# Two products of a dense SiLU layer computed transposed, with 512 moving columns, through DRAM scratch and transposing loads, with one pool of eight PSUM banks

## The chip, the cores and the metric

One core of a Trainium2 chip. The time is the device time of one execution in microseconds (us); the profile is one such execution, and its span (320.8 us before) is a little shorter than the time (322.6 us), because the time also holds what lies around the traced instructions. PE is TensorE; PEld is its loading of stationary operands; ACT is ScalarE, DVE is VectorE; SP is the engine whose queue issues nearly all DMA transfers of this kernel, in order.

## The reference

```python
def _fwd_reference(x, w1, w2):            # x [1, 2048, 640], w1 [640, 1536], w2 [1536, 640], bf16
    h = jnp.einsum("bsd,df->bsf", x, w1)
    h = _silu(h)
    return jnp.einsum("bsf,fd->bsd", h, w2)

def reference(x, w1, w2, grad_out):       # returns out, grad_x, grad_w1, grad_w2
    _out, _vjp = jax.vjp(_fwd_reference, x, w1, w2)
    return (_out, *_vjp(grad_out))
```

There are six matrix products: h = x w1, g = grad_out w2^T, out = silu(h) w2, grad_x = gh w1^T, grad_w2 and grad_w1.

## The kernel before

The sequence is worked through in four chunks of 512 rows. In a chunk, h and g are computed transposed (F on the partitions, 512 rows of the sequence moving), giving `aT` and `ghT`. Then `sd_phase` makes out and grad_x of the chunk: a 128x128 piece of `aT` or `ghT` is stationary and 320 columns of `w2` or of `w1` transposed move. At the end two phases compute the weight gradients from `a_blk` and `gh_blk`, which are `aT` and `ghT` written to DRAM scratch and loaded back transposed.

```python
    P = 128                                # S, D, F = 2048, 640, 1536
    SC, FC, DH = 512, 512, D // 2          # ST, DT, FT = 16, 5, 12 blocks of 128
    abpool = ...                           # bufs=1: a_blk 0
    ps_h = ctx.enter_context(tc.tile_pool(name="ps_h", bufs=4, space=PSUM))   # one bank each
    ps_o = ctx.enter_context(tc.tile_pool(name="ps_o", bufs=2, space=PSUM))   # two banks each
    # ... first loads; 36 warm-up matmuls; chunk 0 of x is transposed on PE ...

        def sd_phase(c, lhs_all, rhs_all, dst_v, on_act):
            o_sb = opool.tile([P, STC, D], dt_in, name="o_sb")
            for sl in range(STC):                              # 4 blocks of rows
                op_ = ps_o.tile([P, 2, 512], FP32, name="op")
                for ft in range(FT):                           # 12
                    for hf in range(2):
                        nc.tensor.matmul(
                            op_[:, hf, 0:DH],
                            lhsT=lhs_all[:, ft, sl * P:(sl + 1) * P],
                            rhs=rhs_all[:, ft, hf * DH:(hf + 1) * DH],
                            start=(ft == 0), stop=(ft == FT - 1),
                        )
                # evicted by ACT (out) or DVE (grad_x) to o_sb
            nc.sync.dma_start(out=dst_v[:, c * STC:(c + 1) * STC, :], in_=o_sb[:])

        for c in range(NCH):
            # ... h and g groups, 5 matmuls of 512 columns each, 12 + 12 groups ...
            # aT, ghT -> aT_scr, ghT_scr
            if c == NCH - 1:
                load_a_blk(0, abpool)                          # transposing load
            sd_phase(c, aT, w2_nat, out_v, True)
            sd_phase(c, ghT, w1T, gx_v, False)

    with ExitStack() as fctx:                                  # last phases
        # fpool, gbpool, s1pool, ab2pool, in this order
        for fc in range(1, NFC):
            load_a_blk(fc, ab2pool)
        # three transposing loads of gh_blk, then grad_w2 (240 matmuls) and grad_w1
```

Of the kernel before, what the change touches and what calls it, by code (L numbers as in the profile page):

```python
# [8 lines left out]
ACT = mybir.ActivationFunctionType  # L9
ALU = mybir.AluOpType  # L10
FP32 = mybir.dt.float32
# [4 lines left out]
def kernel(  # L16
# [11 lines left out]
    nc = tc.nc  # L28
    P = 128
# [6 lines left out]
    S, D = x2.shape  # L36
    F = w1.shape[1]
    ST, DT, FT = S // P, D // P, F // P
    SC = 512
    NCH = S // SC  # L40
    STC = SC // P
    DH = D // 2
    FC = 512
    NFC = F // FC
    LAG = 2
    NWARM = 36
    dt_in = x.dtype

    dram = ctx.enter_context(tc.tile_pool(name="dram", bufs=1, space=bass.MemoryType.DRAM))
    natpool = ctx.enter_context(tc.tile_pool(name="natpool", bufs=1))  # L50
    abpool = ctx.enter_context(tc.tile_pool(name="abpool", bufs=1))
    ps_h = ctx.enter_context(tc.tile_pool(name="ps_h", bufs=4, space=bass.MemoryType.PSUM))
    ps_o = ctx.enter_context(tc.tile_pool(name="ps_o", bufs=2, space=bass.MemoryType.PSUM))

    aT_scr = dram.tile([F, S], dt_in, name="aT_scr")
    ghT_scr = dram.tile([F, S], dt_in, name="ghT_scr")
    g2T_scr = dram.tile([D, F], dt_in, name="g2T_scr")

    go_nat = natpool.tile([P, ST, D], dt_in, name="go_nat")
# [6 lines left out]
    out_v = out2.rearrange("(st p) d -> p st d", p=P)  # L66
    gx_v = gx2.rearrange("(st p) d -> p st d", p=P)

    a_blks = []

    def load_a_blk(fc, pool):
        a_blk = pool.tile([P, ST, FC], dt_in, name="a_blk")
        nc.sync.dma_start_transpose(out=a_blk[:], in_=aT_scr[fc * FC:(fc + 1) * FC, :])
        a_blks.append(a_blk)

    with ExitStack() as mctx:
        cpool = mctx.enter_context(tc.tile_pool(name="cpool", bufs=1))
        wpool = mctx.enter_context(tc.tile_pool(name="wpool", bufs=1))
# [3 lines left out]
        opool = mctx.enter_context(tc.tile_pool(name="opool", bufs=2))  # L82
# [9 lines left out]
        ident = cpool.tile([P, P], dt_in, name="ident")  # L92
        make_identity(nc, ident[:])

        w1_nat = wpool.tile([P, DT, F], dt_in, name="w1_nat")
        w2_nat = wpool.tile([P, FT, D], dt_in, name="w2_nat")
        w1T = wpool.tile([P, FT, D], dt_in, name="w1T")
        w2T = wpool.tile([P, DT, F], dt_in, name="w2T")

        def load_xT(c):  # L100
            xT = xpool.tile([P, DT, SC], dt_in, name="xT")
            nc.sync.dma_start_transpose(out=xT[:], in_=x2[c * SC:(c + 1) * SC, :])
            return xT

        def load_goT(c):
            goT = xpool.tile([P, DT, SC], dt_in, name="goT")
            nc.sync.dma_start_transpose(out=goT[:], in_=go2[c * SC:(c + 1) * SC, :])
            return goT
# [51 lines left out]
        def g_group(ft, goT, ghT):  # L160
            gp = ps_h.tile([P, SC], FP32, name="hp")
            for dt_ in range(DT):
                nc.tensor.matmul(  # L163
                    gp[:],
                    lhsT=w2T[:, dt_, ft * P:(ft + 1) * P],
                    rhs=goT[:, dt_, :],
                    start=(dt_ == 0),
                    stop=(dt_ == DT - 1),
                )
            nc.vector.scalar_tensor_tensor(  # L170
                out=ghT[:, ft, :], in0=ghT[:, ft, :], scalar=1.0, in1=gp[:], op0=ALU.add, op1=ALU.mult
            )

        def sd_phase(c, lhs_all, rhs_all, dst_v, on_act):
            o_sb = opool.tile([P, STC, D], dt_in, name="o_sb")
            for sl in range(STC):
                op_ = ps_o.tile([P, 2, 512], FP32, name="op")
                for ft in range(FT):
                    for hf in range(2):
                        nc.tensor.matmul(  # L180
                            op_[:, hf, 0:DH],
                            lhsT=lhs_all[:, ft, sl * P:(sl + 1) * P],
                            rhs=rhs_all[:, ft, hf * DH:(hf + 1) * DH],
                            start=(ft == 0),
                            stop=(ft == FT - 1),
                        )
                dst = o_sb[:, sl, :].rearrange("p (h d) -> p h d", h=2)
                if on_act:
                    nc.scalar.activation(dst, op_[:, :, 0:DH], ACT.Copy)  # L189
                else:  # L190
                    nc.vector.tensor_copy(out=dst, in_=op_[:, :, 0:DH])  # L191
            nc.sync.dma_start(out=dst_v[:, c * STC:(c + 1) * STC, :], in_=o_sb[:])

        for c in range(NCH):
            xT, goT = xT_next, goT_next
            aT = apool.tile([P, FT, SC], dt_in, name="aT")
            ghT = apool.tile([P, FT, SC], dt_in, name="ghT")

            if c + 1 < NCH:
                xT_next = load_xT(c + 1)  # L200
                goT_next = load_goT(c + 1)
            if c == 1:
                for j in range(0, ST, STC):
                    nc.sync.dma_start(out=go_nat[:, j:j + STC, :], in_=go_v[:, j:j + STC, :])
            if c == 2:
                for j in range(STC, ST, STC):
                    nc.sync.dma_start(out=x_nat[:, j:j + STC, :], in_=x_v[:, j:j + STC, :])

            if c == 0:
                for ft in range(FT):  # L210
                    h_group(ft, xT, aT, ghT)
                nc.sync.dma_start(
                    out=aT_scr[:, c * SC:(c + 1) * SC].rearrange("(ft p) s -> p ft s", p=P), in_=aT[:]
                )
                sd_phase(c, aT, w2_nat, out_v, True)
                for ft in range(FT):
                    g_group(ft, goT, ghT)
                nc.sync.dma_start(
                    out=ghT_scr[:, c * SC:(c + 1) * SC].rearrange("(ft p) s -> p ft s", p=P), in_=ghT[:]
                )  # L220
                sd_phase(c, ghT, w1T, gx_v, False)
                continue

            for i in range(FT + LAG):
                if i < FT:
                    h_group(i, xT, aT, ghT)
                if i >= LAG:
                    g_group(i - LAG, goT, ghT)

            nc.sync.dma_start(  # L230
                out=aT_scr[:, c * SC:(c + 1) * SC].rearrange("(ft p) s -> p ft s", p=P), in_=aT[:]
            )
            nc.sync.dma_start(
                out=ghT_scr[:, c * SC:(c + 1) * SC].rearrange("(ft p) s -> p ft s", p=P), in_=ghT[:]
            )
            if c == NCH - 1:
                load_a_blk(0, abpool)

            sd_phase(c, aT, w2_nat, out_v, True)
            sd_phase(c, ghT, w1T, gx_v, False)  # L240

    with ExitStack() as fctx:
        fpool = fctx.enter_context(tc.tile_pool(name="fpool", bufs=NFC))
        gbpool = fctx.enter_context(tc.tile_pool(name="gbpool", bufs=NFC))
        s1pool = fctx.enter_context(tc.tile_pool(name="s1pool", bufs=3))

        ab2pool = fctx.enter_context(tc.tile_pool(name="ab2pool", bufs=NFC - 1))
        for fc in range(1, NFC):
            load_a_blk(fc, ab2pool)
        gh_blks = []  # L250
        for fc in range(NFC):
            gh_blk = gbpool.tile([P, ST, FC], dt_in, name="gh_blk")
            nc.sync.dma_start_transpose(out=gh_blk[:], in_=ghT_scr[fc * FC:(fc + 1) * FC, :])
            gh_blks.append(gh_blk)

        gw2_v = gw2.rearrange("(ft p) d -> p ft d", p=P)
        g2T_v = g2T_scr[:].rearrange("(dt p) f -> p dt f", p=P)
# [2 lines left out]
        for fc in range(NFC):  # L260
            a_blk = a_blks[fc]
            g2T = fpool.tile([P, DT, FC], dt_in, name="g2T")
            for dt_ in range(DT):
                gp = ps_h.tile([P, FC], FP32, name="hp")
                for st in range(ST):
                    nc.tensor.matmul(  # L266
                        gp[:],
                        lhsT=go_nat[:, st, dt_ * P:(dt_ + 1) * P],
                        rhs=a_blk[:, st, :],
                        start=(st == 0),  # L270
                        stop=(st == ST - 1),
# [15 lines left out]
        for fc in range(NFC):  # L287
            gh_blk = gh_blks[fc]
            for dt_ in range(DT):
                if dt_ == DT // 2:  # L290
                    store_gw2(fc)
                if fc == NFC - 1 and dt_ == DT - 1:
                    for k, (lo, hi) in enumerate(((0, FC - P), (FC - P, FC))):
                        gp = ps_h.tile([P, FC], FP32, name="hp")
                        for st in range(ST):
                            nc.tensor.matmul(  # L296
                                gp[:, lo:hi],
                                lhsT=x_nat[:, st, dt_ * P:(dt_ + 1) * P],
                                rhs=gh_blk[:, st, lo:hi],
                                start=(st == 0),  # L300
                                stop=(st == ST - 1),
# [4 lines left out]
                        else:  # L306
                            nc.vector.tensor_copy(out=g1[:, lo:hi], in_=gp[:, lo:hi])  # L307
                        nc.sync.dma_start(
                            out=gw1_v[:, dt_, fc * FC + lo:fc * FC + hi], in_=g1[:, lo:hi]
# [3 lines left out]
                for st in range(ST):  # L313
                    nc.tensor.matmul(  # L314
                        gp[:],
                        lhsT=x_nat[:, st, dt_ * P:(dt_ + 1) * P],
                        rhs=gh_blk[:, st, :],
                        start=(st == 0),
                        stop=(st == ST - 1),
# [38 lines left out]
```

## Time and profile before

| | before |
|---|---|
| time, median of the runs beside the prediction | 322.56 us (322.50 to 322.58, 4 runs) |
| span of the profile | 320.8 us |
| PE busy | 317.0 us, 99% |
| PE in the chain that ended last | 98% |
| DMA queue, share of 16 engines | 68.2% |

The page of the profile of the kernel before: span, busy time of the engines, the DMA queue, and one of the two groups of matmuls that the change touches (the other, of grad_x, shows the same numbers; busy time, then the mean of one in ns, then the idle time before them), with one group of 512 columns beside them.

```profile
span 320.8 us, 4127 instructions
...
PE 317.0 (99%) x1800; PEld 174.9 (55%) x1800; DVE 104.0 (32%) x179; ACT 75.3 (23%) x132; POOL 0.7 (0%) x6
...
q1 hardware_dynamic: 123200, 55.97, 68.2%
...
L180 PE MATMUL op<-w_nat,aT 128*128 128x320 bf16 x384 | 52.8, 299 | 0.0
...
L266 PE MATMUL hp<-a_blk,go_nat 128*128 128x512 bf16 x240 | 52.0, 379 | 0.0
```

PE has no idle time before these groups. The means, 299 and 379 ns, are the time from issue to end of one matmul; several are under way at once, so they must not be multiplied by a count. 768 x 299 ns would be 230 us, over twice what those matmuls took. The busy time of a group divided by its count (52.0 us / 240 = 217 ns) is near the spacing, and the chain gives it more cleanly.

The chain that ended last of the kernel before, in order of time: start, length, what.

```profile
0.74 4.32 DMA x_nat<-in_x_dram
...
5.11 1.30 PE tp L118 x20
6.40 13.11 PE hp L144 x60
19.51 13.04 PE op L180 x96
32.55 12.95 PE hp L163 x60
45.50 13.04 PE op L180 x96
...
188.40 26.08 PE op L180 x192
214.48 51.80 PE hp L266 x240
266.28 48.35 PE hp L314 x224
314.63 3.51 PE hp L296 x32
318.13 0.04 DVEq L307
```

Each piece begins where the one before it ends. 13.04 us / 96 = 135.8 ns for 320 columns; 51.80 us / 240 = 215.8 ns for 512. Per column that is 0.424 and 0.422 ns.

The Trainium skill, "Trainium Kernel Development and Optimization", section "Performance Expectations", warns that matmul busy time is a bad measure of the distance to the roofline, because matmuls are pipelined. Here the busy sum did not mislead, since PE's 99% agrees with its 98% of the chain.

SP's timeline of the kernel before, from the last chunk on: start, how long SP was held by the issue, engine, line, transfer. A transposing load of 2 MB holds SP for some 7.5 to 10.5 us.

```profile
192.88 10.32 SPq L73 DMA_TRANSPOSE a_blk<-aT_scr  x1
...
214.51 7.51 SPq L73 DMA_TRANSPOSE a_blk<-aT_scr  x1
...
222.70 10.54 SPq L73 DMA_TRANSPOSE a_blk<-aT_scr  x1
233.28 25.43 SPq L253 DMA_TRANSPOSE gh_blk<-ghT_scr  x3
258.88 1.02 SPq L278 DMA_DIRECT2D g2T_scr<-g2T  x2
```

The last gh_blk has been issued at 258.7, and PE needs the first of the three only at 266.3. This is where more DMA work could hurt.

### The profile page before, as it was taken

How to read it: one execution, taken by the hardware profiler on the slowest of the kernel's cores; microseconds unless marked ns; L12 is line 12 of the kernel's file. 1: busy time of each engine (PE TensorE's matmuls, PEld its weight loads, DVE VectorE, ACT ScalarE, POOL GpSimd, SP SyncE). 2: the span in 40 equal slices, each digit the busy share in tenths (PEclk: the TensorE clock that was granted, in tenths of full speed). 3: DMA queues.
4: the chain of work that ended last, by engine and by line, in shares of the span. 5: the costliest groups of instructions: out<-in, count | busy, mean ns of one | idle time of the engine just before them, and what ended most of it. 6: DMA issues, size and time to landing. Idle time of an engine off the chain costs nothing.

```text
span 320.8 us, 4127 instructions
## 1 busy us (share of the span) xinstructions
PE 317.0 (99%) x1800; PEld 174.9 (55%) x1800; DVE 104.0 (32%) x179; ACT 75.3 (23%) x132; POOL 0.7 (0%) x6
## 2 busy tenths in 40 slices
PE   8999999999999999999999999999999999999996
PEld 7467457544577644477754457764444444444443
DVE  1860553577501277810357750120000100110001
ACT  3961000455120055411044521000100001000100
POOL 0000000000000000000000000000000000000000
PEclk9999999999999999999999999999999999999999
DMA  7999999997795020191020079809999999851011
GB/s 232 316 201 207 216 270 244 359 290 272 188 301 152 0 84 0 68 324 58 28 82 0 0 242 266 232 15 298 213 267 253 268 256 231 253 164 47 33 39 45
DMA packets 123218, 56.24 MB, mean 175 GB/s; under 512 B 91712, under 2 KB 123200, under 8 KB 123200
## 3 DMA queue, kind: packets, MB, share of 16 engines
q1 hardware_dynamic: 123200, 55.97, 68.2%
q8 instruction: 14, 0.23, 0.3%
q14 instruction: 4, 0.03, 0.0%
HBM read 9.18 MB, written 23.72 MB: 103 GB/s over the span
## 4 chain that ended last, share of the span: by engine, by line
PE 98%; DMA 1%; DVE 0%; issue 0%; DVEq 0%
PE op L180 33%; PE hp L144 16%; PE hp L266 16%; PE hp L163 16%; PE hp L314 15%; DMA x_nat<-in_x_dram 1%; PE hp L296 1%; PE tp L118 0%; DVE g_2613 L307 0%; DVEq L307 0%
## 5 line engine op out<-in xcount | busy, mean ns | idle before, releaser
L163 PE MATMUL hp<-goT,w2T 128*128 128x512 bf16 x240 | 56.9, 379 | 0.0
L144 PE MATMUL hp<-xT,w_nat 128*128 128x512 bf16 x240 | 56.9, 379 | 0.0
L180 PE MATMUL op<-w_nat,aT 128*128 128x320 bf16 x384 | 52.8, 299 | 0.0
L180 PE MATMUL op<-w1T,ghT 128*128 128x320 bf16 x384 | 52.8, 299 | 0.0
L266 PE MATMUL hp<-a_blk,go_nat 128*128 128x512 bf16 x240 | 52.0, 379 | 0.0
L314 PE MATMUL hp<-gh_blk,x_nat 128*128 128x512 bf16 x224 | 48.5, 379 | 0.0
L151 ACT ACTIVATE aT<-hp 128x512 bf16<-128x512 f32 x48 | 28.7, 597 | 83.0 <-PE hp L144 83.0
L180 PEld LDWEIGHTS <-aT 128*128 128x128 bf16 x384 | 37.6, 98 | 15.2
L180 PEld LDWEIGHTS <-ghT 128*128 128x128 bf16 x384 | 37.6, 98 | 14.7
L266 PEld LDWEIGHTS <-go_nat 128*128 128x128 bf16 x240 | 23.5, 98 | 28.2
L163 PEld LDWEIGHTS <-w2T 128*128 128x128 bf16 x240 | 23.5, 98 | 28.2
L191 DVE CAST o_sb<-op 128x640 bf16<-128x640 f32 x16 | 13.2, 825 | 78.6 <-PE op L180 78.6
L144 PEld LDWEIGHTS <-w_nat 128*128 128x128 bf16 x240 | 23.5, 98 | 27.7
L170 DVE SCALAR_TENSOR_TENSOR ghT<-ghT,hp 128x512 bf16<-128x512 bf16 x48 | 32.5, 682 | 16.2 <-PE hp L163 16.2
L314 PEld LDWEIGHTS <-x_nat 128*128 128x128 bf16 x224 | 21.9, 98 | 26.4
L156 DVE SCALAR_TENSOR_TENSOR ghT<-aT,v 128x512 bf16<-128x512 bf16 x48 | 33.0, 688 | 0.6
L153 ACT ACTIVATE t<-hp 128x512 f32<-128x512 f32 x48 | 28.4, 591 | 0.0
L155 DVE TENSOR_SCALAR v<-t 128x512 bf16<-128x512 f32 x48 | 20.5, 427 | 20.4 <-ACT t L153 20.4
L189 ACT ACTIVATE o_sb<-op 128x640 bf16<-128x640 f32 x16 | 11.3, 704 | 49.1 <-PE op L180 49.1
L276 DVE CAST g2T<-hp 128x512 bf16<-128x512 f32 x7 | 4.8, 692 | 43.4 <-PE hp L266 43.4
L274 ACT ACTIVATE g2T<-hp 128x512 bf16<-128x512 f32 x8 | 4.8, 597 | 60.0 <-PE hp L266 60.0
L90 PE MATMUL wp<-warm 128*128 128x128 bf16 x36 | 4.0, 313 | 1.0 <-DVE warm L85 1.0
(32 smaller groups left out, 27.0 us busy)
## 6 DMA issues: line engine op xcount, KB each, us to landing
aT_scr<-aT SPq DMA_DIRECT2D x4, 1536.0 KB, 6.3
ghT_scr<-ghT SPq DMA_DIRECT2D x4, 1536.0 KB, 10.1
out_dram<-o_sb SPq DMA_DIRECT2D x8, 640.0 KB, 4.5
x_nat<-in_x_dram SPq DMA_DIRECT2D x4, 640.0 KB, 5.5
go_nat<-in_grad_out_dram SPq DMA_DIRECT2D x4, 640.0 KB, 6.9
w_nat<-in_w_dram SPq DMA_DIRECT2D x2, 960.0 KB, 11.2
g2T_scr<-g2T SPq DMA_DIRECT2D x3, 640.0 KB, 4.7
w_nat<-in_w_dram SPq DMA_DIRECT2D x2, 640.0 KB, 7.5
```

The lines of the kernel that those rows point to most:

```text
L144: nc.tensor.matmul(hp[:], lhsT=w1_nat[:, dt_, ft * P:(ft + 1) * P], rhs=xT[:, dt_, :], start=(dt_ == 0), stop=(dt_ == DT - 1),)
L151: nc.scalar.activation(aT[:, ft, :], hp[:], ACT.Silu)
L153: nc.scalar.activation(t[:], hp[:], ACT.Tanh, scale=0.5)
L155: nc.vector.tensor_scalar(out=v[:], in0=t[:], scalar1=-0.5, scalar2=0.5, op0=ALU.mult, op1=ALU.add)
L156: nc.vector.scalar_tensor_tensor(out=ghT[:, ft, :], in0=aT[:, ft, :], scalar=1.0, in1=v[:], op0=ALU.subtract, op1=ALU.mult)
L163: nc.tensor.matmul(gp[:], lhsT=w2T[:, dt_, ft * P:(ft + 1) * P], rhs=goT[:, dt_, :], start=(dt_ == 0), stop=(dt_ == DT - 1),)
L170: nc.vector.scalar_tensor_tensor(out=ghT[:, ft, :], in0=ghT[:, ft, :], scalar=1.0, in1=gp[:], op0=ALU.add, op1=ALU.mult)
L180: nc.tensor.matmul(op_[:, hf, 0:DH], lhsT=lhs_all[:, ft, sl * P:(sl + 1) * P], rhs=rhs_all[:, ft, hf * DH:(hf + 1) * DH], start=(ft == 0), ...
L189: nc.scalar.activation(dst, op_[:, :, 0:DH], ACT.Copy)
L191: nc.vector.tensor_copy(out=dst, in_=op_[:, :, 0:DH])
L266: nc.tensor.matmul(gp[:], lhsT=go_nat[:, st, dt_ * P:(dt_ + 1) * P], rhs=a_blk[:, st, :], start=(st == 0), stop=(st == ST - 1),)
L314: nc.tensor.matmul(gp[:], lhsT=x_nat[:, st, dt_ * P:(dt_ + 1) * P], rhs=gh_blk[:, st, :], start=(st == 0), stop=(st == ST - 1),)
```

## The change

The intent: fewer and longer matmuls. In out and grad_x the operands swap roles. A block of `w2` (or of `w1` transposed) is stationary, and 512 rows of the sequence move, so 768 matmuls of 320 columns become 480 of 512. The results come out transposed; each goes to DRAM scratch, is loaded back by a transposing load and stored. All matmuls now draw from one pool of eight PSUM banks. Memory is made for the new tiles by giving `a_blk` 0 the place of `w1_nat`, and by a new order of the last pools.

```diff
-    abpool = ctx.enter_context(tc.tile_pool(name="abpool", bufs=1))
-    ps_h = ctx.enter_context(tc.tile_pool(name="ps_h", bufs=4, space=bass.MemoryType.PSUM))
-    ps_o = ctx.enter_context(tc.tile_pool(name="ps_o", bufs=2, space=bass.MemoryType.PSUM))
+    w1pool = ctx.enter_context(tc.tile_pool(name="w1pool", bufs=1))
+    ps_h = ctx.enter_context(tc.tile_pool(name="ps_h", bufs=8, space=bass.MemoryType.PSUM))
+    oT_scr = dram.tile([D, S], dt_in, name="oT_scr")
+    gxT_scr = dram.tile([D, S], dt_in, name="gxT_scr")
+    def store_rows(c, pool):
+        for scr, dst_v in ((oT_scr, out_v), (gxT_scr, gx_v)):
+            o_sb = pool.tile([P, STC, D], dt_in, name="o_sb")
+            nc.sync.dma_start_transpose(out=o_sb[:], in_=scr[:, c * SC:(c + 1) * SC])
+            nc.sync.dma_start(out=dst_v[:, c * STC:(c + 1) * STC, :], in_=o_sb[:])
# ... cut: w1_nat moves to w1pool, and a_blk 0 takes its place there ...
+        def sd_phase(c, w_all, rhs_all, scr):
+            oT = opool.tile([P, DT, SC], dt_in, name="oT")
+            for dt_ in range(DT):
+                op_ = ps_h.tile([P, SC], FP32, name="hp")
+                for ft in range(FT):
+                    nc.tensor.matmul(
+                        op_[:],
+                        lhsT=w_all[:, ft, dt_ * P:(dt_ + 1) * P],
+                        rhs=rhs_all[:, ft, :],
+                        start=(ft == 0), stop=(ft == FT - 1),
+                    )
# ... evicted by ACT and DVE in turn; oT goes to scr ...
+            store_rows(c - 1, opool)              # after the h and g groups of chunk c
-        fpool, gbpool, s1pool, ab2pool            # (order of the last pools, shortened)
+        ab2pool, gbpool, fpool, s1pool
+        store_rows(NCH - 1, s1pool)               # after the loads of a_blk and gh_blk
```

More of the change, by code (lines that the diff above doesn't have):

```diff
@@ L67, with load_a_blk @@
     gx_v = gx2.rearrange("(st p) d -> p st d", p=P)
+    def store_rows(c, pool):
[3 more added lines that the diff above has]
+            nc.sync.dma_start(out=dst_v[:, c * STC:(c + 1) * STC, :], in_=o_sb[:])
     a_blks = []
-    def load_a_blk(fc, pool):
-        a_blk = pool.tile([P, ST, FC], dt_in, name="a_blk")
+    def load_a_blk(fc, pool, tag=None):
+        a_blk = pool.tile([P, ST, FC], dt_in, name="a_blk", tag=tag or "a_blk")
         nc.sync.dma_start_transpose(out=a_blk[:], in_=aT_scr[fc * FC:(fc + 1) * FC, :])
@@ L93 @@
         make_identity(nc, ident[:])
-        w1_nat = wpool.tile([P, DT, F], dt_in, name="w1_nat")
+        w1_nat = w1pool.tile([P, DT, F], dt_in, name="w1_nat", tag="w1a")
+        w2T = wpool.tile([P, DT, F], dt_in, name="w2T")
         w2_nat = wpool.tile([P, FT, D], dt_in, name="w2_nat")
         w1T = wpool.tile([P, FT, D], dt_in, name="w1T")
-        w2T = wpool.tile([P, DT, F], dt_in, name="w2T")
         def load_xT(c):
@@ L172, in g_group @@
             )
-        def sd_phase(c, lhs_all, rhs_all, dst_v, on_act):
-            o_sb = opool.tile([P, STC, D], dt_in, name="o_sb")
-            for sl in range(STC):
-                op_ = ps_o.tile([P, 2, 512], FP32, name="op")
+        def sd_phase(c, w_all, rhs_all, scr):
+            oT = opool.tile([P, DT, SC], dt_in, name="oT")
+            for dt_ in range(DT):
+                op_ = ps_h.tile([P, SC], FP32, name="hp")
                 for ft in range(FT):
-                    for hf in range(2):
-                        nc.tensor.matmul(
-                            op_[:, hf, 0:DH],
-                            lhsT=lhs_all[:, ft, sl * P:(sl + 1) * P],
-                            rhs=rhs_all[:, ft, hf * DH:(hf + 1) * DH],
-                            start=(ft == 0),
-                            stop=(ft == FT - 1),
-                        )
-                dst = o_sb[:, sl, :].rearrange("p (h d) -> p h d", h=2)
-                if on_act:
-                    nc.scalar.activation(dst, op_[:, :, 0:DH], ACT.Copy)
-                else:
-                    nc.vector.tensor_copy(out=dst, in_=op_[:, :, 0:DH])
-            nc.sync.dma_start(out=dst_v[:, c * STC:(c + 1) * STC, :], in_=o_sb[:])
+                    nc.tensor.matmul(
+                        op_[:],
+                        lhsT=w_all[:, ft, dt_ * P:(dt_ + 1) * P],
+                        rhs=rhs_all[:, ft, :],
+                        start=(ft == 0),
+                        stop=(ft == FT - 1),
+                    )
+                if dt_ % 2 == 0:
+                    nc.scalar.activation(oT[:, dt_, :], op_[:], ACT.Copy)
+                else:
+                    nc.vector.tensor_copy(out=oT[:, dt_, :], in_=op_[:])
+            nc.sync.dma_start(
+                out=scr[:, c * SC:(c + 1) * SC].rearrange("(dt p) s -> p dt s", p=P), in_=oT[:]
+            )
         for c in range(NCH):
@@ L214 @@
                 )
-                sd_phase(c, aT, w2_nat, out_v, True)
+                sd_phase(c, w2_nat, aT, oT_scr)
                 for ft in range(FT):
@@ L220 @@
                 )
-                sd_phase(c, ghT, w1T, gx_v, False)
+                sd_phase(c, w1T, ghT, gxT_scr)
                 continue
@@ L236 @@
             if c == NCH - 1:
-                load_a_blk(0, abpool)
-            sd_phase(c, aT, w2_nat, out_v, True)
-            sd_phase(c, ghT, w1T, gx_v, False)
+                load_a_blk(0, w1pool, "w1a")
+            sd_phase(c, w2_nat, aT, oT_scr)
+            sd_phase(c, w1T, ghT, gxT_scr)
     with ExitStack() as fctx:
+        ab2pool = fctx.enter_context(tc.tile_pool(name="ab2pool", bufs=NFC - 1))
+        gbpool = fctx.enter_context(tc.tile_pool(name="gbpool", bufs=NFC))
         fpool = fctx.enter_context(tc.tile_pool(name="fpool", bufs=NFC))
-        gbpool = fctx.enter_context(tc.tile_pool(name="gbpool", bufs=NFC))
         s1pool = fctx.enter_context(tc.tile_pool(name="s1pool", bufs=3))
-        ab2pool = fctx.enter_context(tc.tile_pool(name="ab2pool", bufs=NFC - 1))
         for fc in range(1, NFC):
```

## The prediction

> **What bounds it now.** TensorE: on the page PE is busy 317.0 of 320.8 us, and PE is 98% of the chain that ended last; the rest is 4.3 us of the first load and the tail after the last matmul (318.1 to 320.8). The chain in order of time has no gap between PE's pieces; the table of stretches shows the granted clock at 1.00. So only the number of matmuls times their spacing counts. I take the spacing from the chain (the group means, 379 and 299 ns, are latencies of pipelined matmuls and would promise 48 us that are not there): 240 matmuls of 512 columns in 51.80 us = 215.8 ns; 96 of 320 columns in 13.04 us = 135.8 ns. Both are columns / 2.4 GHz plus 2.5 ns, as the Trainium skill, "TensorE: Matmul & The Clock Gate", section "Wait — 56ns, not 53.3ns?", states. So 320 columns already ran at full column rate, and the change saves only the fixed 2.5 ns of each matmul done away with. Weight loads (98 ns) hide under either.
>
> **What changes.**
> - PE: 768 x 135.8 ns = 104.3 us become 480 x 215.8 ns = 103.6 us: 0.7 us gained, all on the critical path. The columns streamed are equal.
> - Evictions: 16 ACT (704 ns) + 16 DVE (825 ns) become 24 + 16 of 128x512, at the 597 and 692 ns of such copies in the last phase: 25.4 us for 24.5 us, on engines 23% and 32% busy. Off the path.
> - PSUM: eight shared banks for four plus two pairs. PE never waited for a bank, so nothing is won; a bank returns eight groups later (over 8 us), so nothing is lost.
> - DMA: each 640 KB result goes to scratch, is loaded transposed (5 to 6 us to landing, as the g2 loads show) and stored: 8 more transposing loads and stores on SP's in-order queue. The DMA share is 0.1 to 0.3 from 100 us to 180 us. SP will be held some 20 us longer near 70 to 100 us by waits for landings, moving chunk 3's xT from 81 to perhaps 100 us, needed only at 162.
> - Last chunk: its transposing loads and stores stand behind all a_blk and gh_blk loads, which PE waits for, so they delay only the g2T and g1 stores. The new pool order gives time back: a_blk 1 waits about for the end of the out phase (near 202), no longer for that of grad_x (214.5). Before, SP caught up with the g1 stores near 288 us; 295 to 300 now, well before the end.
>
> **Prediction.** 322.57 - 0.7 = 321.85 us. 8 in 10: 321.3 to 322.9 us. Faster by over 2%: 1%; within 2%: 96.5%; slower: 2.5%.
>
> **What would show it right or wrong.** The chain: out and grad_x phases of 12.95 us (60 x 215.8) instead of 13.04; all other phases unchanged; no gaps. PE matmuls 1512 instead of 1800. SP's timeline: a_blk 1 issued near 203 us; gh_blk 0 landed before 265 us; g1 stores caught up with PE before 305 us. DMA queue share up from 68% to some 78%.
>
> **What would make it wrong.** A chunk's load held by SP's in-order waits beyond its need (a PE gap released by a DMA at 110 or 162 us); gh_blk late (a gap at 266 us or later); last stores not caught up (tail over 2.7 us); weight loads of w2 or w1T not hidden; a lower clock under the denser stream.

## The result, and the profile after

| | before | after |
|---|---|---|
| time, first series (4 runs each) | 322.56 us (322.50 to 322.58) | 322.04 us (321.72 to 322.44) |
| ratio, first series | | 0.9985, 95% interval 0.9968 to 1.0002 |
| time, second series (9 and 5 runs) | 322.89 us (322.56 to 323.13) | 321.87 us (321.67 to 321.99) |
| ratio, second series | | 0.9967, 95% interval 0.9954 to 0.9981 |
| span of the profile | 320.8 us | 320.1 us |
| matmuls | 1800 | 1512 |

A ratio is the mean time of one kernel's fast runs over the mean of the other's fast runs of the same rounds, so it is not quite the ratio of the medians quoted. All four outputs are correct. The gain is far under 2%. The first series alone does not even show it, since its interval reaches over 1; the second series does, and so do the chains below.

The page of the changed kernel, the lines that answer to those of before.

```profile
span 320.1 us, 3590 instructions
...
PE 316.2 (99%) x1512; PEld 146.7 (46%) x1512; DVE 101.9 (32%) x179; ACT 78.3 (24%) x140; POOL 0.7 (0%) x6
...
q1 hardware_dynamic: 149184, 66.46, 81.8%
...
L186 PE MATMUL hp<-aT,w_nat 128*128 128x512 bf16 x240 | 52.5, 379 | 0.0
...
L276 PE MATMUL hp<-a_blk,go_nat 128*128 128x512 bf16 x240 | 52.0, 379 | 0.0
```

The count fell by 288, and the busy time of PE by 0.8 us. The busy share of PEld fell from 55% to 46%, and the time hardly moved: the weight loads were hidden before and are hidden now.

The chain of the changed kernel.

```profile
0.74 4.51 DMA x_nat<-in_x_dram
...
5.30 1.29 PE tp L125 x20
6.59 12.95 PE hp L151 x60
19.54 12.95 PE hp L186 x60
32.49 12.95 PE hp L170 x60
45.44 12.95 PE hp L186 x60
...
187.89 25.90 PE hp L186 x120
213.79 51.80 PE hp L276 x240
265.59 48.35 PE hp L324 x224
313.94 3.51 PE hp L306 x32
317.44 0.04 DVEq L317
```

Each out or grad_x phase went from 13.04 to 12.95 us, and there are eight of them: 0.7 us. Nothing else in the chain changed but the first 20 us, which is a matter of its own (below, at e5), and there is still no gap. (The 13.11 and 12.95 us of the first h phase differ only in where the chain cuts overlapping matmuls: from the start of its first matmul to that of the first out matmul it is 12.95 us in both.)

SP's timeline of the changed kernel from the last chunk on.

```profile
191.49 11.05 SPq L80 DMA_TRANSPOSE a_blk<-aT_scr  x1
203.07 0.38 SPq L197 DMA_DIRECT2D oT_scr<-oT  x1
213.86 7.54 SPq L80 DMA_TRANSPOSE a_blk<-aT_scr  x1
...
222.07 9.44 SPq L80 DMA_TRANSPOSE a_blk<-aT_scr  x1
231.61 24.85 SPq L261 DMA_TRANSPOSE gh_blk<-ghT_scr  x3
256.56 2.87 SPq L73 DMA_TRANSPOSE o_sb<-oT_scr  x1
259.47 3.80 SPq L73 DMA_TRANSPOSE o_sb<-gxT_scr  x1
263.38 2.24 SPq L74 DMA_DIRECT2D out_dram<-o_sb  x2
265.73 1.83 SPq L288 DMA_DIRECT2D g2T_scr<-g2T  x2
```

The loads that PE waits for stand where they stood. The new round trip of the last chunk begins behind them, holds SP for 9.1 us (256.6 to 265.7), and pushes only stores back. One line is not as predicted: the second a_blk is issued at 213.9, at the end of grad_x, and not near 203. SP's waits of the changed kernel between 185 and 240 us name what held it (L186 is the line of the out and grad_x matmuls; us in all, times, longest):

```profile
SPq L80 <- PE hp L186: 19.8, 2, 10.4
```

The longest wait lasts from 203.5 to the last grad_x matmul.

### The profile page after: what moved, and what is told of

It is laid out like the page before. It is cut to its first block, busy times and chain, and to the rows that moved or that the text cites. A ratio compares the mean times of both kernels' runs of the same rounds, so it can differ in the third digit from the quotient of the medians.

```text
span 320.1 us, 3590 instructions
## 1 busy us (share of the span) xinstructions
PE 316.2 (99%) x1512; PEld 146.7 (46%) x1512; DVE 101.9 (32%) x179; ACT 78.3 (24%) x140; POOL 0.7 (0%) x6
## 3 DMA queue, kind: packets, MB, share of 16 engines
q1 hardware_dynamic: 149184, 66.46, 81.8%
## 4 chain that ended last, share of the span: by engine, by line
PE 98%; DMA 1%; DVE 0%; issue 0%; DVEq 0%
PE hp L186 32%; PE hp L151 16%; PE hp L276 16%; PE hp L170 16%; PE hp L324 15%; DMA x_nat<-in_x_dram 1%; PE hp L306 1%; PE tp L125 0%; DVE g_2364 L317 0%; DVEq L317 0%
## 5 line engine op out<-in xcount | busy, mean ns | idle before, releaser
L186 PE MATMUL hp<-aT,w_nat 128*128 128x512 bf16 x240 | 52.5, 379 | 0.0
L186 PE MATMUL hp<-ghT,w1T 128*128 128x512 bf16 x240 | 52.5, 379 | 0.0
L194 ACT ACTIVATE oT<-hp 128x512 bf16<-128x512 f32 x24 | 14.3, 597 | 110.0 <-PE hp L186 110.0
L186 PEld LDWEIGHTS <-w_nat 128*128 128x128 bf16 x240 | 23.5, 98 | 28.3
L186 PEld LDWEIGHTS <-w1T 128*128 128x128 bf16 x240 | 23.4, 98 | 28.4
L151 PEld LDWEIGHTS <-w_nat 128*128 128x128 bf16 x240 | 23.4, 98 | 28.1
L196 DVE CAST oT<-hp 128x512 bf16<-128x512 f32 x16 | 11.1, 692 | 78.0 <-PE hp L186 78.0
```

Of the source, the lines that this page charges most:

```text
L151: nc.tensor.matmul(hp[:], lhsT=w1_nat[:, dt_, ft * P:(ft + 1) * P], rhs=xT[:, dt_, :], start=(dt_ == 0), stop=(dt_ == DT - 1),)
L186: nc.tensor.matmul(op_[:], lhsT=w_all[:, ft, dt_ * P:(dt_ + 1) * P], rhs=rhs_all[:, ft, :], start=(ft == 0), stop=(ft == FT - 1),)
L194: nc.scalar.activation(oT[:, dt_, :], op_[:], ACT.Copy)
L196: nc.vector.tensor_copy(out=oT[:, dt_, :], in_=op_[:])
```

## The experiments

Two theories of the result stood against each other. The first is the prediction's: each matmul costs its columns at full rate plus about 2.5 ns, and the gain is 288 times that, with nothing else on the path. The rivals: the gain is the banks' or the pools' (A), or it is larger and the extra DMA traffic eats part of it (B). The first series fed B: it showed only 0.5 us, and the changed kernel scattered by 0.7 us where before scattered by 0.1.

Eleven experiments ran, one of them (e5) the changed kernel again; e1 to e4, e5 to e8 and e9 to e11 ran on three different chips, each group with the kernel before beside it. The times of all of them scatter by 0.3 to 1.1 us (one, e8, by 3.4 us), which is as much as the effect, so the profiles decide. In the profile the scatter can be cut off: I count PE's time from the first out matmul to the end of the last matmul (in the lines of before above, 318.13 - 19.51 = 298.62). Taken from start to start of these two matmuls, the traces give 298.55 us before and 297.83 after, the same difference of 0.72 us, so it does not hang on the modelled ends.

### e1: everything but the form of the matmuls

```diff
-            for dt_ in range(DT):                  # 5 x 12 matmuls of 512 columns
+            for sl in range(STC):                  # 4 x 12 x 2 matmuls of 320 columns, two banks
# ... stored to the same scratch; out and grad_x are wrong on purpose
```

> Everything of the change except the form of the matmuls: shared eight banks, scratch, transposing loads, new pools stay; out and grad_x are again 768 matmuls of 320 columns (the two outputs come out wrong on purpose). Theory (288 matmuls fewer, 2.5 ns each): the gain is lost, PE pieces of 13.04 us per phase again, time equal to the kernel before, 322.5 +- 0.2. Rival A (the gain comes from the banks or the pools): it stays at about 322.0, 0.5 below before. Rival B (the extra DMA traffic costs something that hides part of the gain): above before, 322.7 or more.

Measured: 322.85 us, and before 322.85 in the same rounds; ratio 0.9999 (0.9987 to 1.0012). The absolute 322.5 +- 0.2 was missed, and 322.85 taken alone would have counted for B; but the kernel before stood as high in these rounds, so only the comparison with it counts. The lines of e1's chain from the warm-up on, with the first out phase and the end:

```profile
0.99 4.02 PE wp L97 x36
...
20.03 13.04 PE hp L188 x96
...
315.14 3.51 PE hp L306 x32
```

From the first out matmul to the last: 318.65 - 20.03 = 298.62 us, to 0.01 us that of before. The gain goes away with the matmuls, although the banks, the pools and the extra DMA traffic stay. That refutes A and B in this size.

### e2: the new matmuls without the round trip

```diff
-            nc.sync.dma_start_transpose(out=o_sb[:], in_=scr[:, c * SC:(c + 1) * SC])
-            nc.sync.dma_start(out=dst_v[:, c * STC:(c + 1) * STC, :], in_=o_sb[:])
# ... oT is stored straight into the output's bytes, in wrong order on purpose
```

> The new matmuls, but no scratch and no transposing loads for out and grad_x: each oT tile is stored straight into the output's bytes in wrong order on purpose. Theory: the traffic is off the critical path, so the same time as the changed kernel, 321.8 to 322.1, phases of 12.95 us. Rival B (traffic costs the 0.2 us that are missing to the predicted gain and makes the runs scatter by 0.7 us): 321.6 or lower, and the runs agree within 0.15 us as those of before do.

Measured: 322.04 us, ratio to before 0.9976 (0.9963 to 0.9988); the runs went from 321.70 to 322.48. From the first out matmul to the last: 317.18 - 19.28 = 297.90 us, exactly as in the changed kernel (317.44 - 19.54). The transposing loads cost nothing, and the scatter stays without them. B falls.

### e3 and e4: the same columns in more matmuls

```diff
-                for ft in range(FT):
-                    nc.tensor.matmul(op_[:], lhsT=..., rhs=rhs_all[:, ft, :], ...)
+                for q in range(0, SC, 256):        # e4: 128
+                    for ft in range(FT):
+                        nc.tensor.matmul(op_[:, q:q + 256], lhsT=..., rhs=rhs_all[:, ft, q:q + 256], ...)
```

(A form with the loops the other way round starts a group of sums in a bank in which another one is still open.)

> The changed kernel with its 480 matmuls of 512 columns each cut into two of 256 (same columns, same outputs). Theory of 2.5 ns fixed per matmul: 109.2 ns each, phases of 13.10 us, 1.2 us more than the changed kernel, about 323.2. Rival (a weight load of 98 ns plus its own fixed cost no longer hides under 109 ns): more than 324.

> The same cut into four of 128 columns: 1920 matmuls. Theory: 53.3 + 2.5 = 55.8 ns each, phases of 13.4 us, 3.6 us more than the changed kernel, about 325.6. Rival (each matmul needs its own weight load, and a pair takes about 81 ns as the Trainium skill, TensorE: Matmul & The Clock Gate, section Back-to-back issue gap, states for 128 columns): 48 us more, about 374.

Measured: 323.13 us and 325.66 us; both outputs are correct. The chain of e3, out and grad_x of the last chunk (those of chunks 1 and 2 are as long; in e4 the two phases of chunk 0 hold one pause each and are 0.2 us longer):

```profile
189.35 26.20 PE hp L187 x240
```

and the same of e4:

```profile
190.75 26.80 PE hp L187 x480
```

With those of before and after this is the law of the case, measured in one place of one kernel:

| columns of a matmul | chain | spacing | columns / 2.4 GHz | rest |
|---|---|---|---|---|
| 512 | 25.90 us / 120 | 215.8 ns | 213.3 ns | 2.5 ns |
| 320 | 26.08 us / 192 | 135.8 ns | 133.3 ns | 2.5 ns |
| 256 | 26.20 us / 240 | 109.2 ns | 106.7 ns | 2.5 ns |
| 128 | 26.80 us / 480 | 55.8 ns | 53.3 ns | 2.5 ns |

From 128 to 512 columns the spacing grows by 160.0 ns, which is 0.4167 ns per column, that is 2.4 GHz at one column per cycle; so the 2.4 GHz and the 2.5 ns both come out of these rows.

Even at 128 columns, where each matmul has a weight load of its own, the loads stay hidden. Their recorded 98 ns is a latency too, since one follows each 55.8 ns. The Trainium skill, "TensorE: Matmul & The Clock Gate", section "Back-to-back issue gap", gives about 81 ns for 128 columns and about 131 ns for 512 as sustained rates with weight loads; these runs show 55.8 and 215.8, so the rival built on that section falls. The page's own formula for an isolated matmul fits to 0.1 ns.

### e5: the changed kernel again

No edit.

> The changed kernel unaltered, timed again in five rounds, because its first runs scattered by 0.7 us where those of before agreed within 0.1 us, and on another occasion before scattered as much. Theory: 0.6 to 0.8 us under before (ratio 0.9976 to 0.9981), and the same scatter in both, since it comes from the first microseconds[...], which the change does not touch: runs with the lower mean granted clock are the longer ones. Rival (the extra DMA traffic makes the changed kernel scatter and eats part of the gain): before agrees within 0.2 us, the changed kernel does not, ratio 0.9985 or more.

Measured: 321.87 us beside 322.89, ratio 0.9967 (0.9954 to 0.9981). This is a little more gain than expected (0.9976 to 0.9981), and the scatter is the other way round from the first series: now before spreads by 0.6 us and the changed kernel by 0.3. So scatter does not belong to either kernel. The part of the expectation about the mean granted clock held only loosely: the shortest run of the changed kernel here is its one run with 1.000, the longest of before its one with 0.999, but in e6 and e7 the longest run has 1.000. From the first out matmul to the last: 317.55 - 19.64 = 297.91 us again.

Where the scatter lies, the profiles show. Chunk 0 of x is transposed by 20 matmuls on PE right after the warm-up. These are the lines of the chains of e5 and of e1:

```profile
5.06 1.62 PE tp L125 x20
```

```profile
5.04 2.04 PE tp L125 x20
```

In twelve of the thirteen profiles (in e11 a wait for x parts them) these 20 took between 1.28 and 2.08 us, in seven of them over 1.6. The starts of the single matmuls in the traces show why. The 36 warm-up matmuls, of 128 columns too, follow each other every 107 ns in all profiles, but for the last few in e4 and e10. In the seven slow profiles the first transposes do so as well; then the spacing falls to 56 ns, that of e4's 128 columns, and stays there. In e5 six of the 19 spacings are 106 to 107 ns and the last eleven 55 to 56; in e1 fourteen and three. The fall comes at 4.1 us at the earliest (e4) and at 6.8 us at the latest (e3). Fourteen times 51 ns are 0.7 us: so most of the 0.8 us is the moment at which TensorE passes from half rate to full rate, which differs from run to run and which the change does not touch. That much is shown.

For the cause, the Trainium skill, "TensorE: Matmul & The Clock Gate", section "What's actually happening", says that TensorE starts at half clock, 1.2 GHz, and is released by a free-running window of about 3.4 us of activity, so that the moment varies between runs. At 1.2 GHz 128 columns would take 106.7 ns (an estimate from that page's figure), and the 107 ns fit it. But that the clock is the cause is not shown: the granted clock in the records of these stretches reads 1.00 at either rate, and no run changed the warm-up.

### e6: one pool of eight banks alone

```diff
-    ps_h = ... bufs=4;  ps_o = ... bufs=2 pairs
+    ps_h = ... bufs=8
-                op_ = ps_o.tile([P, 2, 512], FP32, name="op")
+                ops = [ps_h.tile([P, SC], FP32, name="hp") for _ in range(2)]
# ... matmuls as before; the two tiles are evicted one by one
```

> The kernel before with one pool of eight banks for all matmuls and nothing else: each 128x640 pair of banks becomes two tiles of one bank, evicted one by one. Theory (PE never waited for a bank): same as before within 0.15 us. Rival A (part of the gain is the banks'): 0.3 to 0.7 us faster than before.

Measured: 322.89 us beside 322.89, ratio 0.9998 (0.9985 to 1.0010); 318.43 - 19.80 = 298.63 us. The banks are worth nothing here, because PE never waited for one. The interval of the times alone (-0.5 to +0.3 us) would still leave room for a part of A; the stretch does not. A falls in this direct form too.

### e7 and e8: how much slack the round trip has

```diff
-        store_rows(NCH - 1, s1pool)
+        for _ in range(2):                         # e8: 4
+            store_rows(NCH - 1, s1pool)
```

> The changed kernel with the last chunk's two transposing loads and stores done twice, to see how much slack stands behind the loads that PE needs. They held SP for 9.1 us (256.6 to 265.7) and SP caught up with the g1 stores at about 297. Theory: caught up near 306, PE without gap, tail as before, time as the changed kernel within 0.3 us. Rival (the last chunk's round trip is already near the critical path): 2 us or more.

> The same done four times: SP is held 27 us longer, first g1 store near 296 or later, the g2 loads and stores behind it. Theory: PE still without gap (three g1 buffers and eight banks hold eleven groups of 3.45 us, until 303), but the stores no longer catch up before PE ends at 317.4, so the tail grows: 2 to 7 us more than the changed kernel. Rival: nothing up to here, or a gap of PE.

e7 measured 322.34 us, 0.5 above the changed kernel's median of the same rounds where 0.3 was allowed. Its transposes at the start took 1.81 us, and its end after the last matmul 3.0 us in place of 2.7; between, 317.71 - 19.81 = 297.90 us, and SP had caught up with the g1 stores at about 304. So PE was not touched; at most the 0.3 us of tail are the second round trip's.

e8 measured 328.97 us (328.2 to 331.6), 7.1 us above the changed kernel, just over the 2 to 7 expected. The table of stretches of e8 (length, busy time and instructions of PE, PEld, DVE, ACT, POOL, then clock, DMA share and GB/s):

```profile
300.00:317.60 17.60, 17.60 (x97) 8.70 (x95) 3.12 (x5) 2.39 (x4) 0.00 (x0) 1.00 1.08 268
317.60:326.40 8.80, 0.02 (x1) 0.00 (x0) 1.28 (x3) 1.09 (x2) 0.00 (x0) 0.62 0.63 198
```

PE works without a gap that the table shows (from start to start its stretch is 0.16 us longer) to the end of its work at 317.6, hardly later than in the changed kernel (317.4), and then 8.8 us follow in which stores that SP could not issue earlier are written. One further round trip costs 0.3 us of tail at most; three more are paid as a tail. The change's own one stands well inside.

### e9: the second a_blk freed from its late wait

```diff
-        w2T = wpool.tile([P, DT, F], dt_in, name="w2T")
+        w2T = w1pool.tile([P, DT, F], dt_in, name="w2T", tag="w2a")
+                load_a_blk(1, w1pool, "w2a")       # right behind a_blk 0
```

> The changed kernel waited with a_blk 1 until the end of the last grad_x phase, which the prediction had missed. Here a_blk 1 gets w2T's place in the pool that lives on, so that it needs only the last g matmul (about 188). Theory: its load is issued right behind a_blk 0, near 203 us, the g1 stores catch up with PE some 7 to 11 us earlier than in the changed kernel (near 287 to 290), PE's pieces are the same to 0.05 us and the time is that of the changed kernel within 0.3 us. Rival (the late a_blk 1 costs PE something that the chain hides): 0.3 us or more faster.

Measured: 322.23 us, ratio to before 0.9977 (0.9962 to 0.9992). SP's timeline of e9:

```profile
192.13 20.00 SPq L80 DMA_TRANSPOSE a_blk<-aT_scr  x2
```

Both loads are out by 212.1, SP catches up with the g1 stores at about 284 instead of 297 (287 to 290 were expected), and PE needs 318.09 - 20.18 = 297.91 us, as before the edit. So the late wait was there, can be taken away, and is worth nothing.

### e10 and e11: the first microseconds

```diff
-        nc.sync.dma_start(out=x_nat[:, 0:STC, :], in_=x_v[:, 0:STC, :])
-        nc.sync.dma_start(out=w1_nat[:, :, 0:FH], in_=w1_v[:, :, 0:FH])
+        nc.sync.dma_start(out=x_nat[:, 0:2, :], in_=x_v[:, 0:2, :])
+        nc.sync.dma_start(out=x_nat[:, 2:STC, :], in_=x_v[:, 2:STC, :])
+        nc.sync.dma_start(out=w1_nat[:, :, 0:P], in_=w1_v[:, :, 0:P])     # e11: nc.scalar
# ... the rest of the first w1 block likewise; transposes in two halves
```

> A try at the only stretch left over, the first 6.6 us: the changed kernel with chunk 0 of x loaded in two halves, its transposes done half by half, and the first weights 128 columns wide. Theory: PE starts to transpose about 1 us earlier, but [...] the first matmuls wait for the weights behind x: 0 to 0.6 us faster than the changed kernel, scatter about as before.

> The same with the first two weight loads issued from ACT's queue at once, beside x on SP's queue. Theory: weights no longer wait behind x, but the bytes share the same engines, so x lands later: within 0.4 us of the run with halves. If the issue itself (0.5 us each on SP) was what bound, 0.5 us or more faster than it.

Measured: 322.72 us (ratio to before 1.0001) and 322.23 us (0.9986), that is no better than the changed kernel, and e10 rather worse. In e10 PE began to transpose at 4.71 instead of 5.30, but then waited for the second piece of weights, which landed at 7.8. In e11 the second half of x landed only at 6.6, where in e10 the transposes of both halves were done by 6.0. The chain of e10:

```profile
2.26 5.58 DMA w_nat<-in_w_dram
...
7.88 12.04 PE hp L152 x55
```

The expectation of e10 (0 to 0.6 us faster) was wrong. What binds there stays open: e11 came 0.5 us under e10, where its theory (the bytes) allowed 0.4 and its rival (the issue on SP) asked for 0.5 or more, and each of the two scatters by 1 us. No version beat the changed kernel.

## Why the prediction was right, point by point

- Size of the gain. Predicted 0.7 us from 288 x 2.5 ns. In the profiles, from the first out matmul to the last: 298.62 us before, 297.90 after, 0.72 us. e1 and e6, with the old matmuls, show 298.62 and 298.63; e2, e5, e7 and e9, with the new ones, 297.90 to 297.91. This is shown.
- Time. Predicted 321.85 us, measured 322.04 and, repeated, 321.87. The difference between the two series is start-up scatter of up to 0.8 us, which the prediction had not reckoned with; the range held it. That 321.87 lies so near to 321.85 is luck: the kernel before stood at 322.89 in those rounds, 0.3 us above the value from which the prediction started.
- PSUM and evictions off the path: right (e6; PE without gaps).
- DMA: the added round trips are off the path, right (e1 and e2). The share of the queue came to 81.8% where some 78% were predicted, which had no effect.
- SP's order: chunk 3's xT was issued at 86.6, 5 us later than before, where "perhaps 100" was feared, and the g1 stores caught up at about 297, within the 295 to 300 predicted.
- Wrong in one step: "a_blk 1 waits about for the end of the out phase (near 202), no longer for that of grad_x (214.5)". It was issued at 213.86 and waited for the last grad_x matmul. I had reasoned from which old tiles lie under the new one. In the built program the wait on that load names the last grad_x matmul, although by its address the tile lies over `w2T` and the first bytes of `w2_nat`, which this matmul does not read. The tile framework thus set a coarser wait than the addresses ask for; a prediction of when a load may start should read the wait itself. e9 shows that the step had no weight.

## What to carry to other kernels

Before making matmuls longer, take their spacing from pieces of the chain that have no gap, and subtract columns / 2.4 GHz; the rest (2.5 ns here, for 128 to 512 columns) times the number of matmuls saved is all there is to win while PE never waits. Neither the mean duration of a matmul nor the busy share of weight loads says so. When an effect is smaller than the scatter of the times, find in the profiles where the scatter lies, and compare a stretch that leaves it out: here a stretch of 298 us repeated to 0.01 us while the times moved by 0.7.

## What the Trainium skill lacked or had wrong

- "TensorE: Matmul & The Clock Gate", section "Back-to-back issue gap": it gives sustained rates with weight loads of about 81 ns (128 columns) and 131 ns (512). These runs show 55.8 and 215.8 ns, with a weight load for every matmul; the formula there that is called isolated (columns / 2.4 + 2.5) fits the sustained stream at 128, 256, 320 and 512 columns.
- The same page, section "Part 4: PE-mode transpose": it gives about 275 ns for a 128x128 transpose inside a kernel and says that the full clock does not engage for transposes. Here the recorded duration of one is 219 ns in the fast stretches and 314 ns in the slow ones, the spacing 56 and 107 ns; in e1 it falls from the slow to the fast one in the midst of the 20 transposes. A transpose costs its spacing, not its duration.
- The same page, section "Why this matters for your kernels": it advises keeping TensorE busy for at least 4 us to get past the start. Here 36 warm-up matmuls filled 4.02 us, and the transposes right behind them still began at half rate in 7 of 13 profiles; the full rate came 3.1 us (e4) to 5.8 us (e3) after the first warm-up matmul, and the recorded granted clock did not show it.
- "Trainium Kernel Development and Optimization", section "Performance Expectations": it names the busy share of weight loads as a good measure. Here it fell from 55% to 46% while the work of PE shrank by 0.2%; for hidden weight loads it says nothing about the distance to the limit.
- No page that I found says how long a large transposing load holds the queue that issues it on this chip: in the changed kernel 7.5 to 11.1 us for 2 MB (24.85 us for three in a row), and 2.3 to 11.7 us for 640 KB.
